# A gated linear-attention kernel with a squareplus MLP: one Softplus for the first gates, fp32 products for three cumulative sums, identity products, output column halves, and a new order table

## The chip, the cores and the metric

The kernel runs on one core of one Trainium2 chip. The metric is device time in microseconds (us) of one execution, lower is better; the time given for a kernel is the median of its runs. Engines in this text: PE is TensorE (PEld its weight loads), DVE is VectorE, ACT is ScalarE, POOL is GpSimd, SP is SyncE.

## The reference

Inputs are q, k, v and f_logit of shape (4, 8, 768, 48) in fp32, and two weight matrices, (384, 2048) and (2048, 384). The first stage is a recurrence per batch and head, the second a two-layer MLP over the 3072 tokens:

```python
f = 1.0 / (1.0 + np.exp(-f_logit))
for t in range(S):
    state = f[:, :, t, :, None] * state + einsum('bhd,bhe->bhde', k[:, :, t], v[:, :, t])
    y[:, :, t] = einsum('bhd,bhde->bhe', q[:, :, t], state)
x = y.transpose(0, 2, 1, 3).reshape(B * S, H * D)
h = x @ w_in
g = 0.5 * (h + np.sqrt(h * h + 4.0))
out = g @ w_out
```

## The kernel before

The 3072 tokens are cut into 12 *pairs* of 256 tokens, numbered 0 to 11, three to a batch. Pair 0 is handled in two *parts* of four heads each (`FINE = [0]`), all others in one part. The work on a pair is a fixed list of *pieces*, each a few instructions, made in `describe` and named by kind, pair and part: `tp2.0` is the transpose piece of pair 2. The names that matter below:

- `lf`, `lq`, `lk`, `lv` load a pair's inputs (384 KB each, SP's queue). `wi0` to `wi3` load a quarter of w_in each, `wo0` to `wo7` an eighth of w_out each, both from POOL's queue with a cast to fp16.
- `ex` and `ln` (L180, L188, ACT): the log of the gate, as ln(1 + exp(-f)), in two passes. `ad` (L194) adds the two tokens that share a partition; `hi` (L198, the helper's cast at L135 or L137) and `lo` (L203) split the sum into two fp16 halves in the tile `hl`; `cu` (L211, L217, PE) forms cumulative sums from the two halves: two products of 384 columns with a triangular matrix, and eight narrow ones of 3 columns that give block sums.
- `c1` (L225, DVE), then `ep` and `ea` (L236, ACT): exponentials of the sums. `ge` (L259, ACT) and `gs` (L264, helper L140): the decay of a whole block, 12 numbers a partition, then a multiplication that zeroes it in the other half of the partitions. `gb` (L271): the decay across two pairs.
- `qm`, `km` (helper L140): q and k scaled by these. `vc`: v in fp16. `tp` (L295, PE) and `te` (L135 or L137): transposes of q and k and their copies out of PSUM, for pairs 0 to 3; later pairs are transposed by DMA (`tx`, L278).
- `sc` (L319), `pm` (L327, DVE): scores and their masking. `kv` (L338), `ia` (L348), `sa`, `sb`: the state. `yt` (L388), `yn` (L397): the output of the recurrence; `yc`, `xp` (L421), `xe`: its cast and transposition into the tile xT.
- `m1` (L436, PE): x times w_in, eight pieces of six products to a pair. `sq` (L445) and `rt` (L450), ACT: square and square root. `gt` (L460, DVE). `m2` (L472, PE): times w_out, eight pieces of four products of 384 columns. `ev` (helper L135 or L137): out of PSUM; `st` (L493): the store.

There is no scheduler at run time. A table, `ORDER`, lists all pieces in one row of words such as `qm2.00:P` or `cu3.0:T@3`: piece, engine (S, A, D, P, T for SP, ACT, DVE, POOL, PE) and for PE the PSUM bank. Every engine runs its pieces in the order of the table, and waits at each for what it reads and for the buffer that it writes. `TABLE:e` and `TABLE:s` load ACT's function table, for exp and ln or for sqrt. The words of a piece tell its engine, so a piece can move from one engine to another through the table alone.

## Time and profile before

| | us |
|---|---|
| median of 3 runs | 189.88 (189.34 to 190.11) |
| profiled execution, whole | 188.35 |
| its span, first to last instruction | 186.6 |
| PE, ACT, DVE, POOL busy | 167.3, 161.1, 145.1, 90.2 |

The profiled execution is 1.53 us shorter than the median. 1.75 us of it lie outside of the span. Busy time counts what an engine was occupied with; a product of PE is pipelined, so its mean duration is longer than the distance from one to the next.

### The profile page before, as it was taken

What the parts mean: (1) busy time and instruction counts of PE and PEld (TensorE: products, weight loads), DVE (VectorE), ACT (ScalarE), POOL (GpSimd) and SP (SyncE); (2) the same over time, 40 slices, a digit from 0 to 9 for tenths busy, and PEclk for the clock granted to TensorE, in tenths of its full rate; (3) what the DMA queues carried; (4) which work ended last, traced back from release to release, by engine and by line L of the source; (5) the groups of instructions that cost most, each with busy time, mean ns of one, the idle gap of its engine ahead of it and who ended that gap; (6) DMA issues with size and microseconds to landing.
All of it is one profiled execution on the core that took longest, in us unless ns stands there. A gap on an engine that the chain in (4) does not pass through costs nothing.

```text
span 186.6 us, 5571 instructions
## 1 busy us (share of the span) xinstructions
PE 167.3 (90%) x2279; PEld 123.0 (66%) x2279; DVE 145.1 (78%) x277; ACT 161.1 (86%) x268; POOL 90.2 (48%) x126
## 2 busy tenths in 40 slices
...
GB/s 132 271 261 246 226 246 247 215 218 211 264 263 208 157 98 286 128 262 175 263 168 215 293 144 97 219 164 128 197 198 132 111 86 0 18 156 169 5 77 92
DMA packets 80506, 32.88 MB, mean 176 GB/s; under 512 B 73888, under 2 KB 80448, under 8 KB 80480
## 3 DMA queue, kind: packets, MB, share of 16 engines
...
q14 instruction: 8, 0.07, 0.1%
HBM read 25.17 MB, written 4.72 MB: 160 GB/s over the span
## 4 chain that ended last, share of the span: by engine, by line
PE 48%; issue 22%; DMA 15%; POOL 6%; SPq 5%; ACT 1%; POOLq 0%
PE ps L436 20%; PE ps L472 18%; DMA q<-in_q_dram 7%; POOL qk L140 4%; DMA qkT<-qk 3%; DMA f<-in_f_logit_dram 3%; SPq L173 3%; DMA k<-in_k_dram 3%; SPq L278 2%; PE ps L319 2%; PE ps L388 2%; PE ps L338 2%; PE ps L211 1%; PE ps L397 1%; PE ps L295 1%
## 5 line engine op out<-in xcount | busy, mean ns | idle before, releaser
L460 DVE SCALAR_TENSOR_TENSOR g<-ps,r 128x512 f16<-128x512 f32 x96 | 62.1, 684 | 17.4 <-ACT r L450 17.2
L436 PE MATMUL ps<-xT,win 128*128 128x256 f16 x576 | 71.2, 273 | 2.7 <-DMA win<-in_moe_w_in_dram 1.8
L472 PE MATMUL ps<-wout,g 128*128 128x384 f16 x384 | 70.8, 326 | 0.0
L436 PEld LDWEIGHTS <-win 128*128 128x128 f16 x576 | 55.0, 98 | 13.3 <-DMA win<-in_moe_w_in_dram 2.0
L445 ACT ACTIVATE hsq<-ps 128x512 f16<-128x512 f32 x96 | 53.6, 603 | 6.5 <-PE ps L436 6.2
L450 ACT ACTIVATE r<-hsq 128x1024 f16<-128x1024 f16 x48 | 50.4, 1063 | 0.8
L472 PEld LDWEIGHTS <-g 128*128 128x128 f16 x384 | 36.0, 98 | 19.7
L327 DVE TENSOR_TENSOR pm<-ps,mask 128x512 f16<-128x512 f32 x48 | 30.3, 683 | 3.2 <-PE ps L319 3.0
L140 POOL TENSOR_TENSOR qk<-k,ep 128x384 f16<-128x384 f32 (+1 forms) x19 | 19.3, 1019 | 18.7 <-PE ps L388 10.5
L140 POOL TENSOR_TENSOR qk<-q,ea 128x384 f16<-128x384 f32 (+1 forms) x19 | 18.7, 990 | 4.0 <-ACT ea L236 2.2
L493 POOL DMA_DIRECT2D out_dram<-os x2 | 1.1, 575 | 39.0 <-ACT os L135 38.4
L211 PE MATMUL ps<-hl,tri 128*128 128x384 f16 (+1 forms) x26 | 7.4, 351 | 8.9 <-DVE hl L137 6.2
L137 POOL CAST v<-v 128x768 f16<-128x768 f32 x9 | 7.8, 862 | 14.2 <-DMA v<-in_v_dram 8.8
L194 POOL TENSOR_TENSOR ss<-s 128x384 f32<-128x384 f32 (+1 forms) x10 | 9.9, 991 | 6.0 <-ACT s L188 5.9
L180 ACT ACTIVATE f<-f 128x768 f32<-128x768 f32 (+1 forms) x13 | 10.3, 802 | 2.8 <-DMA f<-in_f_logit_dram 2.8
L137 DVE COPY os<-ps 128x384 f32<-128x384 f32 (+1 forms) x17 | 8.5, 513 | 2.9 <-PE ps L472 2.9
L203 POOL TENSOR_TENSOR hl<-ss,hl 128x384 f16<-128x384 f32 (+1 forms) x11 | 9.7, 881 | 2.0 <-DVE hl L137 1.8
L188 ACT ACTIVATE s<-f 128x768 f32<-128x768 f32 (+1 forms) x13 | 10.2, 810 | 0.3
L319 PE MATMUL ps<-qkT 48*64 48x128 f16 x384 | 8.8, 227 | 1.6 <-ACT qkT L135 0.7
L137 DVE CAST y<-ps 128x384 f16<-128x384 f32 x15 | 8.1, 551 | 2.2 <-PE ps L397 2.0
L319 PEld LDWEIGHTS <-qkT 48*64 48x64 f16 x384 | 6.4, 111 | 4.9 <-issue 1.9
L135 ACT CAST y<-ps 128x384 f16<-128x384 f32 x9 | 4.2, 475 | 5.2 <-PE ps L397 3.8
...
## 6 DMA issues: line engine op xcount, KB each, us to landing
f<-in_f_logit_dram SPq DMA_DIRECT2D x11, 384.0 KB, 5.5
k<-in_k_dram SPq DMA_DIRECT2D x11, 384.0 KB, 5.0
q<-in_q_dram SPq DMA_DIRECT2D x11, 384.0 KB, 5.5
v<-in_v_dram SPq DMA_DIRECT2D x11, 384.0 KB, 6.4
...
win<-in_moe_w_in_dram POOLq DMA_DIRECT2D x4, 384.0 KB, 7.6
...
```

What stands on the lines that cost most here:

```text
L137: eng(e).tensor_copy(out=o, in_=i)
L140: eng(e).tensor_tensor(out=o, in0=a, in1=b, op=ALU.mult)
L180: nc.scalar.activation(out=t, in_=t, func=AF.Exp, scale=-1.0)
L188: nc.scalar.activation(out=T["s", p][:, :, hs], in_=T["f", p][:, hs].rearrange("p h i d -> p i h d"), func=AF.Ln, bias=1.0)
L194: eng(e).tensor_tensor(out=T["ss", p][:, hs], in0=T["s", p][:, 0, hs], in1=T["s", p][:, 1, hs], op=ALU.add)
L319: nc.tensor.matmul(out=T["sc", p, i, h][64 * cc:64 * cc + 64, j, :], lhsT=t[r, 1, j, i, :], rhs=t[r, 0, j], start=True, stop=True)
L327: eng(e).tensor_tensor(out=T["pm", p, i, h], in0=T["sc", p, i, h], in1=K["mask"][:, i].unsqueeze(1).broadcast_to([128, 4, 128]), op=ALU.mult)
L436: nc.tensor.matmul(out=T["h", p, m][:, a], lhsT=K["win"][m // 2][:, j, m % 2 * 256 + a * 128:m % 2 * 256 + a * 128 + 128], rhs=T["xT", p][ ...
L445: nc.scalar.activation(out=T["hsq", p, r][:, a], in_=T["h", p, m].rearrange("p a c t -> p (a c t)"), func=AF.Square, scale=1.0)
L450: nc.scalar.activation(out=T["r16", p, r], in_=T["hsq", p, r], func=AF.Sqrt, scale=0.25, bias=1.0)
L460: nc.vector.scalar_tensor_tensor(out=T["g", p][:, 2 * m:2 * m + 2, :].rearrange("p a t -> p (a t)"), in0=T["h", p, m].rearrange("p a c t - ...
L472: nc.tensor.matmul(out=T["o", p, cc], lhsT=T["g", p][:, jn, cc * 128:(cc + 1) * 128], rhs=K["wout"][jn // 2][:, jn % 2, :], start=(jn == 0 ...
```

## The change

Seven things, of which the last goes through the whole table:

1. Pairs 0 and 1 (`SOFT`) get the log of the gate by one ACT pass with the function Softplus in place of `ex` and `ln`. This function has a table of its own: the program begins with `TABLE:p`, and loads `TABLE:e` after the passes of these two pairs.
2. Pairs 1, 2 and 3 (`DIRECT`) have no `hi` and `lo`. `ad` writes its fp32 sum into a padded tile s32, and `cu` multiplies that in fp32: one product of 384 columns and four of 3 columns, with fp32 copies of the two constant matrices.
3. `ge` and `gs` become one piece `gs` on ACT with two passes over the same 12 numbers; a bias of 0 or -10000 makes the zeros. `gb` is laid out accordingly.
4. 40 pieces `pw` of four products of the identity with itself (128 columns, fp16) are spread over PE's order, up to the second pair. Nothing reads them.
5. The second 128 tokens of pair 11 are multiplied by w_out in two column halves of 192, each with its own bank, `ev` and two stores; the first 128 have one `ev` and two stores. Stores of pair 11 may go out from ACT's queue as well.
6. An option to mask scores on POOL (`PMACT`) is there, with an empty list.
7. `ORDER` is new throughout, with other engines for some pieces.

```diff
+DIRECT = [1,2,3]
+SOFT = [0,1]
+NS32 = 2
+PMACT = []
+WARM = 40
...
-TABLE:e lf0.1:S lf0.0:S lf1.0:S lq0.0:S lk0.0:S lq0.1:S ex0.1:A lf2.0:S ln0.1:A ex0.0:A ad0.1:P ln0.0:A lk0.1:S ad0.0:D
+TABLE:p lf0.1:S lf0.0:S lf1.0:S lq0.0:S lq0.1:S lk0.0:S pw2:T@0 pw26:T@1 lf2.0:S pw8:T@2 ln0.0:A pw30:T@3 ln0.1:A pw36:T@4
...
+                if p in SOFT:
+                    nc.scalar.activation(out=o, in_=t, func=AF.Softplus, scale=-1.0)
+                else:
+                    nc.scalar.activation(out=o, in_=t, func=AF.Ln, bias=1.0)
...
+                if direct:
+                    o = K["s32"][p % NS32][:, hs, 0:D]
...
+                if direct:
+                    tri, ind, terms = K["tri32"], K["ind32"], [K["s32"][p % NS32]]
+                else:
+                    hl = K["hl"][p % NHL]
+                    tri, ind, terms = K["tri"], K["ind"], [hl[:, 0], hl[:, 1]]
+                z = len(terms) - 1
+                for r, t in enumerate(terms):
+                    nc.tensor.matmul(out=T["cum", p][:, h0 * D:h1 * D], lhsT=tri, rhs=t[:, hs, 0:D], start=(r == 0), stop=(r == z), skip_group_check=True)
...
-            T["gs", p] = sb("gs", p, [128, 3, 4, 2], FP32)
-            mul(e, T["gs", p], T["ge", p].rearrange("p j n -> p n j").unsqueeze(3).broadcast_to([128, 3, 4, 2]),
+            T["gs", p] = sb("gs", p, [128, 2, 4, 3], FP32)
+            for h in range(2):
+                nc.scalar.activation(out=T["gs", p][:, h].rearrange("p j n -> p (j n)"), in_=T["cum", p][:, 384:396], func=AF.Exp, scale=-1.0, bias=K["half"][:, h:h + 1])
...
+        outs = [(0, 0, DM), (1, 0, DM // 2), (1, DM // 2, DM)] if p in SPLIT_OUT else [(0, 0, DM), (1, 0, DM)]
...
+    for i in range(WARM):
+        def pw(e, bk, i=i):
+            t = ps(bk[0], [128, 128], FP32)
+            for n in range(4):
+                nc.tensor.matmul(out=t, lhsT=K["ident"], rhs=K["ident"], start=True, stop=True)
```

Three places of the order. The first is the start of ACT's row, up to the exponentials of pair 0; before (L180 is `ex`, L188 `ln`, L236 `ep` and `ea`, L259 `ge`):

```order
L569 ACT_TABLE_LOAD
L180 ACTIVATE f<-f 128x384
L188 ACTIVATE s<-f 128x2x192
L180 ACTIVATE f<-f 128x384
L188 ACTIVATE s<-f 128x2x192
L180 ACTIVATE f<-f 128x768
L188 ACTIVATE s<-f 128x768
L236 ACTIVATE ep<-ps_152 128x192
```

and after (L192 is Softplus, L142 the cast `hi0.0`, L260 `ep` and `ea`):

```order
L614 ACT_TABLE_LOAD
L192 ACTIVATE s<-f 128x2x192 x2
L142 CAST hl_91<-ss 128x4x48
L192 ACTIVATE s<-f 128x768
L612 ACT_TABLE_LOAD
L260 ACTIVATE ep<-ps_197 128x192 x2
L260 ACTIVATE ea<-cm 128x192
L260 ACTIVATE ep<-cm 128x192
```

Three passes are gone there, a cast and a table load have come in, and the table load stands between the pass over pair 1 and the first exponential of pair 0.

The second is POOL's row from the third load of w_in to `qm2`, where L140 with k or q is `km` and `qm`, L194 `ad3` and `ad4`, L137 and L203 `hi3` and `lo3`; before:

```order
L146 DMA win_110<-in_moe_w_in_dram 128x3x512
L140 TENSOR_TENSOR qk_96<-k,ep 128x4x2x48
L140 TENSOR_TENSOR gb<-gs,ge 128x8
L194 TENSOR_TENSOR ss<-s 128x384 x2
L137 CAST hl_92<-ss 128x8x48
L203 TENSOR_TENSOR hl_92<-ss,hl_92 128x8x48
L146 DMA win_112<-in_moe_w_in_dram 128x3x512
L140 TENSOR_TENSOR qk_97<-k,ep 128x4x2x48
L140 TENSOR_TENSOR gs<-ge,half 128x24 x2
L137 CAST v_602<-v 128x768
L140 TENSOR_TENSOR qk_97<-k,ep 128x4x2x48
L140 TENSOR_TENSOR qk_97<-q,ea 128x4x2x48 x2
```

and after (L147 is the same helper, L153 the load of w_in, L213 `ad4` and then `ad3`, L144 `vc1`):

```order
L147 TENSOR_TENSOR qk_96<-k,ep 128x4x2x48
L153 DMA win_119<-in_moe_w_in_dram 128x3x512
L147 TENSOR_TENSOR qk_96<-q,ea 128x4x2x48
L147 TENSOR_TENSOR qk_96<-k,ep 128x4x2x48
L153 DMA win_118<-in_moe_w_in_dram 128x3x512
L213 TENSOR_TENSOR ss<-s 128x384
L213 TENSOR_TENSOR s_1_106<-s 128x8x48
L147 TENSOR_TENSOR gb<-gs 128x8
L153 DMA win_120<-in_moe_w_in_dram 128x3x512
L147 TENSOR_TENSOR qk_97<-k,ep 128x4x2x48
L144 CAST v_753<-v 128x768
L147 TENSOR_TENSOR qk_97<-k,ep 128x4x2x48
```

`hi3`, `lo3` and two `gs` are gone from between `ad3` and `qm2`, three pieces of pair 1's q and k stand between the loads of w_in, and `ad4` stands ahead of `ad3`.

The third is PE's row around the cumulative sum of pair 1; before:

```order
L211 MATMUL ps_152<-hl_91,tri 128x192
L211 LDWEIGHTS tri
L211 MATMUL ps_193<-hl_92,tri 128x384
L211 LDWEIGHTS tri
L211 MATMUL ps_193<-hl_92,tri 128x384
L217 LDWEIGHTS hl_92
L217 MATMUL ps_193<-ind,hl_92 128x3
```

and after, where L529 is `pw`, and the fp32 products have no weight load of their own in the row:

```order
L529 LDWEIGHTS ident
L529 MATMUL ps_222<-ident 128x128
L236 MATMUL ps_229<-s_1_106,tri_109 128x384
L241 MATMUL ps_229<-ind_111,s_1_106 128x3 x4
L529 LDWEIGHTS ident
L529 MATMUL ps_247<-ident 128x128
```

One wide and four narrow fp32 products stand where two wide and eight narrow ones stood, with identity products on either side.

## Rows read from the trace of the kernel before

**Rows 1.** Busy time by stretch: length; PE, PEld, DVE, ACT, POOL us (instructions); clock, DMA share, GB/s.

```profile
21.00:32.00 11.00, 8.67 (x177) 6.55 (x171) 9.34 (x17) 10.51 (x15) 8.63 (x13) 1.00 1.17 239
32.00:66.00 34.00, 34.00 (x467) 24.73 (x460) 30.31 (x58) 33.85 (x59) 25.83 (x35) 1.00 1.09 217
66.00:72.00 6.00, 5.43 (x123) 3.93 (x124) 5.11 (x10) 5.98 (x11) 2.71 (x4) 1.00 1.16 159
72.00:130.00 58.00, 57.93 (x781) 44.34 (x772) 50.68 (x88) 56.75 (x93) 32.69 (x41) 1.00 0.97 194
130.00:160.00 30.00, 29.04 (x417) 21.02 (x415) 23.28 (x40) 21.26 (x34) 5.62 (x7) 1.00 0.55 115
```

**Rows 2.** The chain that ended last, 16 to 34 us: start, us, what.

```profile
16.80 12.77 DMA q<-in_q_dram
...
29.63 1.96 POOL qk L140 x2
```

**Rows 3.** PE's timeline from 20 us: start, us, instructions, [idle before <-releaser].

```profile
21.07 1.49 PE L436 MATMUL ps<-xT,win 128*128 128x256 f16 x12
...
24.21 1.48 PE L436 MATMUL ps<-xT,win 128*128 128x256 f16 x12 [1.05 <-DMA win<-in_moe_w_in_dram]
...
26.95 1.48 PE L436 MATMUL ps<-xT,win 128*128 128x256 f16 x12 [0.74 <-DMA win<-in_moe_w_in_dram]
...
32.27 1.47 PE L436 MATMUL ps<-xT,win 128*128 128x256 f16 x12
```

**Rows 4.** ACT's timeline: the first passes, and the table load at 23 us.

```profile
6.86 0.84 ACT L180 ACTIVATE f<-f 128x768 f32<-128x768 f32 x1 [1.29 <-DMA f<-in_f_logit_dram]
...
8.48 0.31 ACT L236 ACTIVATE ep<-ps 128x192 f32<-128x192 f32 x1
8.70 0.17 ACT L259 ACTIVATE ge<-ps 128x12 f32<-128x12 f32 x1
...
23.21 1.28 ACT L571 ACT_TABLE_LOAD   x1
24.50 1.06 ACT L450 ACTIVATE r<-hsq 128x1024 f16<-128x1024 f16 x1
```

**Rows 5.** All engines from 11 us, timeline: the masks of pair 0.

```profile
15.15 2.49 DVE L327 TENSOR_TENSOR pm<-ps,mask 128x512 f16<-128x512 f32 x4 [0.47 <-PE ps L319]
```

**Rows 6.** PE's products by form, 9.5 to 17 us: count, busy us, mean ns, idle before.

```profile
L211 PE MATMUL ps<-hl,tri 128*128 128x384 f16 x4 | 1.9, 485 | 2.6 <-ACT hl L135 2.0 <-POOL hl L203 0.6
L217 PE MATMUL ps<-ind,hl 128*128 128x3 f16 x16 | 0.8, 172 | 0.0
```

**Rows 7.** The same, 44 to 62 us.

```profile
L211 PE MATMUL ps<-hl,tri 128*128 128x384 f16 x6 | 1.5, 325 | 0.0
```

**Rows 8.** The chain that ended last, at 44 us: one cumulative sum on PE.

```profile
44.45 0.33 PE ps L211 x2
44.77 0.18 PE ps L217 x8
```

**Rows 9.** POOL's timeline, 12 to 32 us.

```profile
22.23 1.00 POOL L194 TENSOR_TENSOR ss<-s 128x384 f32<-128x384 f32 x1 [1.39 <-ACT s L188]
23.17 0.50 POOL L137 CAST hl<-ss 128x384 f16<-128x384 f32 x1
23.75 0.91 POOL L203 TENSOR_TENSOR hl<-ss,hl 128x384 f16<-128x384 f32 x1
24.61 0.80 POOL L146 DMA_DIRECT2D win<-in_moe_w_in_dram  x1
```

**Rows 10.** DMA issues at 24.6 us: count, KB, us from issue to landing.

```profile
win<-in_moe_w_in_dram POOLq DMA_DIRECT2D x1, 384.0 KB, 6.9
```

**Rows 11.** All engines from 180 us, timeline: the end of the program.

```profile
179.79 2.11 PE L472 MATMUL ps<-wout,g 128*128 128x384 f16 x12
...
181.95 0.62 DVE L137 COPY os<-ps 128x192 f32<-128x192 f32 x2 [0.94 <-PE ps L472]
182.87 0.54 POOL L493 DMA_DIRECT2D out_dram<-os  x1 [0.61 <-DVE os L137]
```

More of the change, by code (lines that the diff above doesn't have):

```diff
@@ L31 @@
-ad2.0:P te0.0.0:A te0.1.1:D c11.0:D wi0:P te0.0.1:A lk2.0:S te0.1.0:D ea1.01:A hi2.0:D sc0.1:T@45 ep1.00:A lo2.0:P ex3.0:A
-sc0.0:T@67 pm0.11:D lv1.0:S wi2:P ea1.00:A cu2.0:T@0 pm0.01:D vc0.0:A pm0.10:D wi1:P ep1.01:A lq2.0:S kv0:T@23 pm0.00:D
-ea2.01:A km1.00:P ln3.0:A c12.0:D yt0:T@57 sa0:D ep2.00:A qm1.01:D ge2:A yn0.1:T yc0.0:A km1.01:D ia0.1:T ge1:A yc0.1:A
-xp0.0:T@4 gb1:P qm1.00:D ep2.01:A xp0.1:T@6 lf5.0:S ad3.0:P xe0.0:D ea2.00:A tp1.0:T@25 xe0.1:D ex4.0:A m1.0.1:T@1 te1.1.0:D
-ln4.0:A m1.0.0:T@7 te1.0.0:D sq0.1:A ad4.0:P sc1.0:T@04 sq0.0:A sc1.1:T@65 pm1.01:D TABLE:s hi3.0:P m1.0.4:T@2 sb0:D lo3.0:P
@@ new lines @@
+ep1.00:A lk2.0:S sc0.1:T@47 vc0.0:P gs0:A vc0.1:A sc0.0:T@16 pm0.10:D cu2.0:T@2 pm0.00:D km1.00:P lv1.0:S pm0.01:D pw39:T@5
+ep2.01:A kv0:T@04 pm0.11:D wi2:P ep1.01:A pw33:T@1 ex3.0:A lq2.0:S c12.0:D yt0:T@56 qm1.00:P sa0:D pw1:T@1 gs2:A gs1:A
+pw9:T@7 yc0.0:D ea2.01:A ia0.1:T km1.01:P yn0.1:T ep2.00:A xp0.0:T@1 yc0.1:D ln3.0:A qm1.01:D wi1:P xp0.1:T@0 xe0.0:A
+tp1.0:T@73 xe0.1:A ea2.00:A pw13:T@2 lf5.0:S te1.0.0:D m1.0.1:T@5 ex4.0:A te1.1.0:D m1.0.0:T@6 sq0.1:A gb1:D pw3:T@1 ln4.0:A
+pw19:T@0 sc1.0:T@27 sq0.0:A sc1.1:T@31 ad4.0:P pm1.00:D pw10:T@0 TABLE:s m1.0.5:T@0 pm1.01:D ad3.0:P m1.0.4:T@2 sb0:D rt0.0:A
@@ new lines @@
+pm1.11:D pw35:T@7 gb2:P cu3.0:T@4 wi3:P lv2.0:S sq0.5:A gt0.1:D km2.01:P sq0.4:A pw15:T@7 pm1.10:D m1.0.3:T@1 rt0.2:A c13.0:D
+m1.0.2:T@5 gt0.0:D vc1.0:P lk3.0:S sq0.3:A pw23:T@7 gt0.5:D pw11:T@3 sq0.2:A pw27:T@7 km2.00:P kv1:T@63 gt0.4:D rt0.1:A
+ia1.0:T lq3.0:S yt1:T@70 qm2.01:P sa1:D TABLE:e yn1.0:T gt0.2:D pw34:T@2 ia1.1:T qm2.00:P yn1.1:T yc1.0:D pw4:T@6 pw21:T@2
+yc1.1:D ep3.00:A xp1.0:T@5 wo1:P tp2.0:T@62 sb1:D ea3.00:A xe1.0:D ep3.01:A wo3:P xp1.1:T@7 te2.1.0:D m1.0.7:T@0 ea3.01:A
+lf7.0:S gs3:A hi4.0:P te2.0.0:D ex5.0:A m1.0.6:T@3 wo0:P xe1.1:D sq0.7:A sc2.0:T@52 gt0.3:D sc2.1:T@46 wo2:P ln5.0:A lf6.0:S
@@ new lines, in describe, with ev @@
+                W.add(f"m2.{p}.{x}{n4}", "T", m2,
+                      reads=[f"g{p}.{2 * n4}", f"g{p}.{2 * n4 + 1}", f"wout{2 * n4}", f"wout{2 * n4 + 1}"] + ([f"o{p}.{x}{n4 - 1}"] if n4 else []),
+                      makes=[f"o{p}.{x}{n4}"], uses=[("g", p)] + ([("bank", f"o{x}.{p}")] if n4 else []),
+                      banks=[f"o{x}.{p}"] if n4 == 0 else [], mode="F", part=(d1 - d0) / DM)
+            def ev(e, bk, x=x, cc=cc, d0=d0, d1=d1, p=p):
+                if ("os", p) not in T:
+                    T["os", p] = sb("os", p, [128, 2, DM], FP32)
+                copy(e, T["os", p][:, cc, d0:d1], T["o", p, x])
```

284 lines of the change are left out of this document (144 added, 140 removed).

## The prediction

> **What bounds the kernel now.** I read the busy time by stretch first [rows 1]. From 32 us on PE is full: 34.00 of 34 us, then 57.93 of 58. Its idle time is 0.57 us at 66 to 72 and 0.96 us at 130 to 160. ACT is nearly as full (33.85 of 34, 56.75 of 58). So the program is three parts: a start in which PE waits, some 150 us in which PE streams at its own pace, and an end behind the last product. A change to the start is worth only what it moves the point from which PE no longer waits.
>
> That point is read from the chain [rows 2] and from PE's timeline [rows 3]. The chain runs over the load of pair 2's q (landed 16.80 + 12.77 = 29.57), two `qm2` on POOL (29.63 + 1.96 = 31.59), on which `tp2.0` on PE waits; the next `m1` at 32.27 starts the stretch without gaps. The other waits of PE are for w_in: 1.05 us ahead of 24.21 and 0.74 us ahead of 26.95. All of these hang on DMA, which moves 239 GB/s at 21 to 32 us [rows 1], and the bytes to be loaded by then are the same in both kernels. I take 32.27 as the mark, and follow each part to it.
>
> **Softplus and its table.** Removed: three `ex` passes of pairs 0 and 1. But ACT stood still for 1.29 us for pair 1's gates, which reach it at 6.86 [rows 4]; what is saved ahead of that is saved from waiting. Behind it comes one pass of 0.84 (the row of `ex` has that; Softplus has no row, taken as equal for the same shape) and then a table load of 1.28: 6.86 + 0.84 + 1.28 = 8.98, where the first exponential stood at 8.48. So pair 0 is 0.5 us later here, not earlier. The row at 23.21 shows that a load costs no more than its 1.28: the next pass starts at 24.50.
>
> The Trainium skill says otherwise (ScalarE: Activation LUTs, section What ACT_TABLE_LOAD costs): a switch costs the load and a drain of about the same length, 2.66 us together. By that the first exponential would stand 1.4 us later still; this trace does not agree, and the sum goes by the row.
>
> **Identity products and the clock.** In the clock column the start reads 1.00 like the rest, but the products say that it ran at the lower level: one of 384 columns took 485 ns at 9.5 to 17 us and 325 at 44 to 62 [rows 6, 7]. The difference, 160 ns, is what 384 columns take more at 1.2 than at 2.4 GHz. PE had done little until then. With 32 identity products ahead of the first sum, and more in the gaps, I expect the full level by about 10 us. On pair 0's path this shortens the transposes behind the last scaled q or k (16 of 64 columns, 0.43 us at 160 ns to 384 columns) and the first half of the scores (about as much). From -0.85, the 0.5 above and the last scaled half of q, now behind another piece on POOL, I keep -0.3 for the first mask, which was at 15.15 [rows 5]. The four masks (2.49) stay.
>
> **fp32 sums.** `hi` and `lo` go for pairs 1 to 3, POOL's being 0.50 + 0.91 for pair 3 [rows 9]. On PE a sum in halves takes 0.33 + 0.18 = 0.51 us [rows 8]. fp32 products have no row. From below: one product for two and four for eight at fp16's pace, 0.25 us. From above: both operands split in two, so four wide and sixteen narrow products, 4 x 0.163 = 0.65, and the narrow ones at the busy time per product that they showed early on, 0.8 / 16 = 0.05 to twice that [rows 6]: 0.65 + 0.8 to 0.65 + 1.6, at most 2.3 us. I take 1.3, near the lower of these two, since the data are twice as wide and the level is then the full one.
>
> The Trainium skill (FP8 and Floating Point Precision, section TensorE Precision Notes) has true fp32 at four passes through the array. By that the wide product alone takes 0.65 us, twice what its two halves take: it speaks against this part of the change, and makes the lower end unlikely. No row here shows it.
>
> Where this falls: pair 2's sum stands between the scores of pair 0 and `kv0`. From about 15.1 us to the end of the masks (14.85 + 2.49 = 17.35) PE has 2.2 us, of which `kv0` and two `pw` take 0.9. Up to 1.3 us it is hidden; beyond, `yt0`, pair 0's casts, and ACT's `ep2` that waits for the sum all move one for one. With 1.3, the first `m1` comes at 20.7 to 21.0 against 21.07 [rows 3].
>
> **21 to 32 us.** Eleven `pw` stand here: 44 products of 128 columns at 0.163 / 3 = 0.054 us, 2.4 us. With `cu3` 0.8 longer that is 3.2 us more work for PE, which was idle for 11.00 - 8.67 = 2.3 us [rows 1]. They lie largely in the waits: three of them (0.65) ahead of the `m1` at 24.21 with its wait of 1.05, `cu3` and two `pw` in that of 0.74 ahead of 26.95. The second does not quite fit; the third quarter of w_in landing a little earlier (less of pair 2's inputs stands ahead of it) pays for it.
>
> POOL decides then. Before, `ad4` began at 22.23, when ACT gave `ln4`, and `hi3`, `lo3` and the issue of `wi3` at 24.61 followed [rows 9]. After, `ad4` stands ahead of `ad3`, and `ln4` on ACT stands behind the first `sq`: I put it about 1 us later, 23.2. Then two sums of 1.00 and a `gb` (0.2): `wi3` at 25.4, that is 0.8 later than 24.61, though 1.4 us of work are gone. It lands 6.9 us after its issue [rows 10], at 32.3, and the `m1` that reads it stood at 32.27. `qm2` ends at 25.4 + 0.8 + five pieces of about 1 us = 31.1 against 31.6. Both sides cancel: **0.0 us at the mark**, with bounds -1.0 (`ln4` on time, `wi3` and `qm2` both 1.4 us of POOL's work earlier, as far as PE's own work lets them) and +1.4 (fp32 at 2.3 us: `cu3` delays the `m1` behind it by 1, and `m1.0.1` is late as well).
>
> **The long stretch.** PE's work from the mark is the same. `gs` on ACT adds twelve short passes of at most 0.17 us [rows 4], 2.0 us; four `yc` casts of 384 columns moved to DVE take 1.2 to 2.5 off (192 columns took 0.31 in the row of `ep`). Taken: 0. The new order can open or close waits like the 0.57 and 0.96 [rows 1]: -1.0 to +1.5.
>
> **The end.** The last piece of PE is now half as wide, with one cast behind it instead of two on DVE, one after the other, 0.62 together [rows 11]: -0.3. The last store is half as large: 0 to -0.3. Taken: -0.35. The product of the columns is split, not enlarged, and costs PE nothing.
>
> **Sum.** 188.35 (the profiled execution) + 0.0 + 0 - 0.35 = 188.0. The median lies 1.53 above that execution; carried over, 189.88 - 0.35 = **189.5 us**.
>
> **The rivals.** *Faster*: POOL's 1.4 us come through, `wi3` is not late, and the mark moves by about -1.0; with the end, and half of the later waits gone (-0.5), 188.0. For it: POOL is on the chain [rows 2], and `hi3`, `lo3` stood ahead of both of its later steps. Against: `ad4` waits for ACT, which is 10.51 of 11 us busy there [rows 1]. *Slower, by the fp32 sums*: they take over 2 us each, so the masks no longer hide pair 2's, and `cu3` holds the `m1` behind it: mark +1.4, end -0.35, 190.9; to 192 if the level of the clock is still the lower at pair 2's. The point is 1.3 us for `cu2`. *Slower, by the order*: waits of 1.5 us or more open in the long stretch, above all where transposes by DMA are waited for: 191.0. *The identity products don't raise the clock* earlier: then they take 0.43 us a piece and stand in front of pair 0's transposes, pair 0 is 0.9 late, and it ends like the second: 190.8.
>
> **How the numbers follow.** Forecast 0.37; faster 0.34; fp32 0.13; order 0.09; clock 0.07. About 0.5% (0.95 us) is what can be told from no change. The forecast's own spread reaches over it at neither end by much, so: faster 0.34, same 0.38, slower 0.28. The range takes in the faster case down to 187.6 and the slower ones to 191.6.
>
> **What would show it.** Right: first exponential at about 9.0; wide fp16 sums at 325 ns already for pair 0; first `m1` within 0.4 us of 21.07; `m1.0.6` or its neighbour at 32.3, behind `wi3`; 4.3 us from the last product to the end. Wrong: `cu2` over 1.3 us with `yt0` behind it; `qm2` ending before 30.5; PE idle by over 2.7 us after 33 us.

## The result, and the profile after

The changed kernel takes **191.84 us** (median of 4 runs, 190.26 to 193.04) against 189.83 (189.34 to 190.11) for the kernel before, run beside it: a ratio of 1.0139, 95% interval 1.0095 to 1.0183. It is slower by 2.0 us; the forecast was 189.5, and the time lies just above its range (187.6 to 191.6). Ratios here and below leave out runs over 1.5% above a kernel's fastest; for two variants (c4_pair1_dve, g1_14_pieces) that leaves out most of them, so there the median of all runs is given too.

The profiled execution took 190.26 us with a span of 188.5 (before 188.35 and 186.6). The loss is there ahead of the mark, the `m1` from which PE no longer waits: it stood at 32.27 [rows 3] and stands at 34.52, +2.25. From the mark to PE's end it was 149.64 us and is 150.00, +0.36. From there to the end of the span it was 4.67 and is 3.97, -0.70. Together +1.91. The profiled execution is the shortest of the four runs; the other three left no trace, so this is the account of the shortest.

The busy time by stretch shows what fills the start. Of before, and then of after (columns as in [rows 1]):

```profile
21.00:32.27 11.27, 8.94 (x180) 6.77 (x175) 9.61 (x17) 10.78 (x16) 8.90 (x14) 1.00 1.16 238
21.07:32.27 11.20, 8.87 (x178) 6.76 (x175) 9.61 (x17) 10.71 (x16) 8.90 (x14) 1.00 1.16 238
32.27:180.00 147.73, 146.12 (x1911) 108.45 (x1909) 120.35 (x212) 133.22 (x217) 66.59 (x84) 1.00 0.83 166
```

```profile
21.00:34.52 13.52, 12.52 (x246) 10.62 (x247) 10.28 (x20) 12.92 (x20) 10.49 (x14) 1.00 1.13 229
22.12:34.52 12.40, 11.68 (x219) 9.93 (x218) 9.77 (x19) 11.80 (x17) 9.96 (x13) 1.00 1.12 227
34.52:180.00 145.48, 144.04 (x1897) 107.31 (x1895) 119.08 (x213) 135.40 (x222) 60.50 (x71) 1.00 0.87 165
```

From 21 us to the mark PE is busy for 12.52 us instead of 8.94, 3.58 more, and idle for 1.00 instead of 2.33. But not all of the 3.58 is added work: most of pair 1's transposes lie behind 21 us now and lay ahead of it before. It is clearer to part the 2.25 at the first `m1`. 1.05 of it arises ahead of the first `m1`, which stands at 22.12 instead of 21.07. The other 1.20 arises between it and the mark, where PE is busy for 11.68 us instead of 8.87, 2.81 more, and idle for 0.72 instead of 2.33: the old waits took in 1.61. PE's timeline of the kernel after (start, us, instructions, idle before; L529 is an identity piece, L236 and L241 the fp32 sums, L314 the transposes, L462 the `m1`, L364 `kv1`):

```profile
9.97 1.72 PE L529 MATMUL ps<-ident 128*128 128x128 f16 x28
...
14.70 0.91 PE L236 MATMUL ps<-s,tri 128*128 128x384 f32 x2
15.45 0.95 PE L241 MATMUL ps<-ind,s 128*128 128x3 f32 x8
16.26 0.38 PE L529 MATMUL ps<-ident 128*128 128x128 f16 x4
...
21.29 0.52 PE L314 MATMUL ps<-ident,qk 64*128 64x64 f16 x24 [1.09 <-DVE qk L147]
21.74 0.40 PE L529 MATMUL ps<-ident 128*128 128x128 f16 x4
22.12 1.47 PE L462 MATMUL ps<-xT,win 128*128 128x256 f16 x12
23.43 0.61 PE L529 MATMUL ps<-ident 128*128 128x128 f16 x8
...
25.65 1.48 PE L462 MATMUL ps<-xT,win 128*128 128x256 f16 x12 [0.72 <-DMA win<-in_moe_w_in_dram]
...
27.20 0.86 PE L236 MATMUL ps<-s,tri 128*128 128x384 f32 x2
27.90 0.95 PE L241 MATMUL ps<-ind,s 128*128 128x3 f32 x8
28.71 0.38 PE L529 MATMUL ps<-ident 128*128 128x128 f16 x4
28.93 1.47 PE L462 MATMUL ps<-xT,win 128*128 128x256 f16 x12
30.24 0.83 PE L529 MATMUL ps<-ident 128*128 128x128 f16 x12
31.00 0.52 PE L364 MATMUL ps<-v,qk 64*128 64x96 f16 x16
...
33.77 0.64 PE L314 MATMUL ps<-ident,qk 64*128 64x64 f16 x32
34.35 0.34 PE L447 MATMUL ps<-ident,y 128*128 128x128 f16 x3
34.52 1.47 PE L462 MATMUL ps<-xT,win 128*128 128x256 f16 x12
```

The identity pieces of the stretch in one row (products by form, 22.12 to 34.52 us, kernel after; count, busy us, mean ns, idle before):

```profile
L529 PE MATMUL ps<-ident 128*128 128x128 f16 x45 | 3.8, 219 | 0.0
```

Three things are to be seen. A sum in fp32 holds PE from 14.70 to 16.26, 1.56 us, where two halves held it for 0.51 [rows 8]; pair 3's holds it from 27.20 to 28.71. Ahead of the first `m1` stands a wait of 1.09 us for pair 1's scaled q. And between the first `m1` and the mark stand identity pieces for which PE never waits; `tp2.0` at 33.77 follows PE's own work, not POOL's `qm2`, which ended at 32.01. The 3.8 us of these pieces is busy time, in which the end of one product overlaps with the start of the next: of PE's row the twelve products at 30.24 take 0.76 us, to 31.00.

How the 1.20 adds up is seen from start to start; before, `kv1` (L338) stood here:

```profile
28.54 0.52 PE L338 MATMUL ps<-v,qk 64*128 64x96 f16 x16
```

The second group of `m1` comes 3.53 us behind the first (before 3.14), since its quarter of w_in landed later. The third comes 3.28 behind the second (before 2.74), with an fp32 sum and two identity pieces in place of a wait of 0.74. `kv1` comes 2.07 behind the third (before 1.59), with the twelve identity products ahead of it and no wait to take them in. From `kv1` to the mark it is 3.52 (before 3.73): the pieces behind `kv1` delayed nothing.

The 1.05 ahead of the first `m1` has two reasons that end together. The wait of 1.09 has its own row. All engines at 19 us, timeline of after:

```profile
19.33 1.90 DVE L147 TENSOR_TENSOR qk<-q,ea 128x384 f16<-128x384 f32 x1
...
19.80 1.00 POOL L147 TENSOR_TENSOR qk<-k,ep 128x384 f16<-128x384 f32 x1
```

DVE's multiplication takes 1.90 us where the same form alone takes 0.55 (rows of e3_pair1_dve below): it ends 0.43 us after POOL's ends. The Trainium skill (GPSIMD Engine Reference, section Specifications) says that POOL's SBUF interfaces are shared with VectorE, with contention where a DVE instruction has two inputs in SBUF. The trace agrees, with 1.90 against 0.55.

The other reason is on ACT. The first `m1` also reads xT, and its copies out of PSUM (`xe`), which DVE made before, are on ACT now, behind the log pass of pair 3 (L194). Before, and then after:

```profile
19.90 0.67 DVE L137 COPY xT<-ps 128x384 f16<-128x384 f16 x2
```

```profile
20.45 0.87 ACT L194 ACTIVATE s<-f 128x768 f32<-128x768 f32 x1
21.19 0.88 ACT L142 COPY xT<-ps 128x384 f16<-128x384 f16 x2
```

They end at 22.07, so without the wait of 1.09 the first `m1` could have started 0.05 us earlier and no more. In c1_win_first and g1_14_pieces below it does wait for these copies. No run moved them back to DVE and nothing else, so what they cost by themselves is not shown.

The end, all engines from 179 us, timeline of after; it answers to [rows 11]:

```profile
183.24 0.36 DVE L144 COPY os<-ps 128x192 f32<-128x192 f32 x1 [1.89 <-PE ps L499]
...
184.56 0.32 ACT L142 COPY os<-ps 128x192 f32<-128x192 f32 x1 [1.83 <-PE ps L499]
184.90 0.50 SPq L517 DMA_DIRECT2D out_dram<-os  x1
```

One cast of 0.32 and one store are left behind the last product (before: 0.62 on DVE, then a store from POOL).

### The profile page after: what moved, and what is told of

Same layout as the page of the kernel before. It is cut to its first block, busy times and chain, and to the rows that moved or that the text cites. A ratio compares the mean times of both kernels' runs of the same rounds, so it can differ in the third digit from the quotient of the medians.

```text
span 188.5 us, 5911 instructions
## 1 busy us (share of the span) xinstructions
PE 177.2 (94%) x2455; PEld 135.0 (72%) x2455; DVE 144.6 (77%) x278; ACT 164.1 (87%) x276; POOL 86.0 (46%) x113
## 4 chain that ended last, share of the span: by engine, by line
PE 31%; ACT 25%; issue 24%; DVE 7%; DMA 6%; POOL 4%; POOLq 0%; SPq 0%; ACTq 0%; DVEq 0%
PE ps L462 11%; PE ps L499 11%; ACT hsq L471 6%; ACT r L476 5%; DMA win<-in_moe_w_in_dram 4%; DVE g L486 3%; ACT ep L260 3%; ACT ea L260 2%; ACT L616 2%; ACT L612 2%; ACT s L194 2%; PE ps L529 2%; ACT f L200 2%; PE ps L236 2%; POOL qk L147 2%
## 5 line engine op out<-in xcount | busy, mean ns | idle before, releaser
L462 PE MATMUL ps<-xT,win 128*128 128x256 f16 x576 | 70.4, 273 | 1.6 <-DMA win<-in_moe_w_in_dram 0.7
L499 PE MATMUL ps<-wout,g 128*128 128x384 f16 (+1 forms) x400 | 70.7, 320 | 0.0
L462 PEld LDWEIGHTS <-win 128*128 128x128 f16 x576 | 55.3, 98 | 11.2 <-issue 1.1
L147 POOL TENSOR_TENSOR qk<-k,ep 128x384 f16<-128x384 f32 (+1 forms) x20 | 19.9, 1001 | 7.5 <-DMA k<-in_k_dram 5.1
L147 POOL TENSOR_TENSOR qk<-q,ea 128x384 f16<-128x384 f32 (+1 forms) x18 | 17.2, 962 | 3.0 <-ACT ea L260 1.8
L529 PE MATMUL ps<-ident 128*128 128x128 f16 x160 | 13.2, 238 | 2.3 <-POOL ident masks.py:199 2.3
L529 PEld LDWEIGHTS <-ident 128*128 128x128 f16 x160 | 11.1, 109 | 2.8 <-POOL ident masks.py:199 2.3
L144 DVE CAST y<-ps 128x384 f16<-128x384 f32 x19 | 10.2, 551 | 2.0 <-PE ps L423 2.0
L147 POOL TENSOR_TENSOR sn<-st,gb 128x384 f16<-128x384 f32 x6 | 5.2, 868 | 14.3 <-DVE st L390 12.8
L147 POOL TENSOR_TENSOR sn<-st,gs 128x384 f16<-128x384 f32 x5 | 4.5, 898 | 14.5 <-DVE st L390 14.5
L144 DVE COPY os<-ps 128x384 f32<-128x384 f32 (+1 forms) x16 | 8.5, 539 | 3.1 <-PE ps L499 2.3
L213 POOL TENSOR_TENSOR ss<-s 128x384 f32<-128x384 f32 (+1 forms) x8 | 7.2, 901 | 6.8 <-ACT s L194 5.1
L142 ACT COPY os<-ps 128x384 f32<-128x384 f32 (+1 forms) x9 | 4.2, 462 | 6.2 <-PE ps L499 6.2
L200 ACT ACTIVATE f<-f 128x768 f32<-128x768 f32 x10 | 8.4, 854 | 1.0 <-DMA f<-in_f_logit_dram 1.0
L338 PE MATMUL ps<-qkT 48*64 48x128 f16 x384 | 8.4, 220 | 0.4 <-DVE g L486 0.4
```

What stands on the lines that cost most here:

```text
L144: eng(e).tensor_copy(out=o, in_=i)
L147: eng(e).tensor_tensor(out=o, in0=a, in1=b, op=ALU.mult)
L200: nc.scalar.activation(out=t, in_=t, func=AF.Exp, scale=-1.0)
L462: nc.tensor.matmul(out=T["h", p, m][:, a], lhsT=K["win"][m // 2][:, j, m % 2 * 256 + a * 128:m % 2 * 256 + a * 128 + 128], rhs=T["xT", p][ ...
L499: nc.tensor.matmul(out=T["o", p, x], lhsT=T["g", p][:, jn, cc * 128:(cc + 1) * 128], rhs=K["wout"][jn // 2][:, jn % 2, d0:d1], start=(jn = ...
L529: nc.tensor.matmul(out=t, lhsT=K["ident"], rhs=K["ident"], start=True, stop=True)
```

## The experiments

Four theories were to be told apart: the *fp32 sums* (1.5 us or more each on PE), the *clock* (whether the identity products raise it, and what they cost where they don't), *Softplus* and its table, and the *order* (handovers, loads, POOL beside DVE). Variants whose names begin with b and f stand on the order of before, the others on the new one.

### Single suspects undone in the kernel after

Loads of w_in, the third and second quarter right behind the first in POOL's order:

```diff
-POOL: wi0 vc0.0 km1.00 wi2 qm1.00 km1.01 wi1
+POOL: wi0 wi2 wi1 vc0.0 km1.00 qm1.00 km1.01
```

> The changed kernel with one change of order: POOL issues wi2 and wi1, the second and third load of w_in, right behind wi0 instead of behind the scalings of pair 1. In the changed kernel they go out at 18.02 and 20.74 us, land at 25.61 and 28.42, and m1.0.5 and m1.0.3 start at 25.65 and 28.93; the mark (first m1 behind tp2.0) is 34.52. Theory LOADS (late issue of w_in sets the mark): they land near 24.2 and 26.9 as before the change, m1.0.5 starts at 24.2, the mark comes to 33.1 and the time falls by about 1.4 us. Theory PE WORK (fp32 sums and identity products fill PE until the mark): m1.0.5 starts earlier, but the mark moves by under 0.5 us, and so does the time.

Measured: 191.59 us, ratio 1.013 (1.007 to 1.0191). The loads were asked for at 14.93 and 15.71 us and nothing was gained: their issue is not the loss. Theory PE WORK is nearer in the time, but the profile doesn't test it, as it differs from the one above in another way. PE's timeline of c1_win_first:

```profile
9.18 1.65 PE L236 MATMUL ps<-s,tri 128*128 128x384 f32 x2 [0.35 <-POOL s L213]
10.62 1.70 PE L241 MATMUL ps<-ind,s 128*128 128x3 f32 x8
12.19 3.15 PE L529 MATMUL ps<-ident 128*128 128x128 f16 x28
...
18.62 0.64 PE L338 MATMUL ps<-qkT 48*64 48x128 f16 x32
```

Here the products show the lower level up to about 17.5 us, although the same 160 identity products run. (The clock column reads 1.00 there, as it does at the start of the kernel before.) The fp32 sum holds PE for 3.01 us (9.18 to 12.19) and the 28 products behind it take 3.15 instead of 1.72; the scores of pair 0 start at 18.62 instead of 14.13, the first `m1` at 25.55, the mark is at 37.33.

The same with two multiplications of pair 1 moved to DVE as well:

```diff
-qm1.00:P km1.01:P
+qm1.00:D km1.01:D
```

> As c1_win_first, and qm1.00 and km1.01 stand on DVE behind qm1.01, as before the change; only km1.00 stays on POOL. In the changed kernel DVE's qm1.01 took 1.90 us (19.33 to 21.23) while POOL worked on km1.01. Theory COLLISION (DVE's scaling waits for POOL's): each of the three takes about 0.55 us, tp1.0 ends by 21.2 instead of 21.8, and m1.0.1 is then set by ACT's xe0.1 alone (22.07); below c1_win_first by 0 to 0.3 us. Theory LOADS: as c1_win_first. If m1.0.1 still starts at 22.1, pair 0's path over ACT is what makes it late.

Measured: 3 of 10 runs at 189.01 to 190.54 (ratio 1.0022, 0.996 to 1.0084), the others at 192.46 to 195.05; the median of all ten is 192.76. This told nothing on the collision, so it was done again without the moved loads (e3, below).

The last 12 identity pieces away:

```diff
-pw13 ... pw21 (12 pieces behind the first transposes of pair 1)
```

> The changed kernel without its last 12 identity pieces (from the transposes of pair 1 on); the 28 ahead of them stay, so the clock rises as early. They take about 0.22 us each on PE, 2.6 us together. Theory PE WORK: the 8 of them between the first m1 and tp2.0 that stand where PE does not wait are gained, the mark falls from 34.52 to about 33.0 and the time by 1.5 us. Theory LOADS: they lie in waits that return; mark and time move by under 0.5 us.

Measured: 191.73 us, 1.0134 (1.0075 to 1.0192), no gain. From the first `m1` to the mark its profile has 11.57 us (24.94 to 36.51) against 12.40 in the kernel after, so without these pieces this stretch is 0.83 us shorter in the profile. That is less than they take of PE's row: waits came back instead, 0.94 us for POOL's `ad3` and 0.78 for DVE's `yc1`, and from `kv1` to the mark it is 3.95 us. But in this execution the level fell back to the lower one from 9.5 to 16.4 us, and the first `m1` came 2.8 us later.

Sums split into fp16 halves again:

```diff
-DIRECT = [1,2,3]
+DIRECT = []
+ad1.0 hi1.0:D lo1.0:P ... ad2.0 hi2.0:D lo2.0:P ... ad3.0 hi3.0:P lo3.0:P
```

> The changed kernel with the sums of pairs 1 to 3 in two fp16 halves again: hi1, hi2 on DVE, lo1, lo2, hi3, lo3 on POOL, each right behind its ad; all else as changed. Theory PE WORK: a sum takes 0.5 us on PE instead of 1.5, so yt0, ep2 and c13 come about 1 us earlier; mark and time fall by 1.0 us or more. Theory LOADS: POOL has 3.7 us more work ahead of wi2, wi1 and wi3, these land later, and the time rises by 1 us or more.

Measured: 191.38 us, 1.0114 (1.0051 to 1.0177). The added `hi1.0` stood ahead of `c10.0` on DVE and held the first exponential to 10.14 us, so this run doesn't price the sums. With `hi1.0` behind `c10.0`, and pair 3's sum ahead of pair 4's:

```diff
-c10.0:D ... te0.0.0:D ... ad4.0:P ad3.0:P
+c10.0:D hi1.0:D lo1.0:P ... te0.0.0:D hi2.0:D ... ad3.0:P hi3.0:P lo3.0:P ad4.0:P
```

> The kernel after with the sums of pairs 1 to 3 split into fp16 halves again, the two steps of pair 1 placed behind the first half of pair 0's prefix copy on VectorE (the earlier variant with split sums had put one ahead of it, which held the first exponential back by about 1.5 us), and the sum of pair 3 prepared ahead of pair 4's. Theory FP32: three sums shorter by 0.9 us each at the full level, of which those of pairs 2 and 3 lie on the path: 190.0 us, ratio 1.003. Theory ORDER: 191.4 us or more, ratio 1.010 or more.

Measured: 191.02 us, 1.0101 (1.007 to 1.0132). By the ratio that is theory ORDER: the fp32 sums are some 0.4 points of the 1.4, but the two intervals overlap.

No identity products at all:

```diff
-pw0 ... pw39
```

> The changed kernel without any identity piece. Theory CLOCK (in the traces so far the full level comes at 5.7 us and stays, or falls again at 9.0 to 9.5, or comes only at 17.5; while it is low, the 28 identity products ahead of pair 0's transposes take 3.15 us instead of 1.72 and pair 0 is up to 4 us late): without them pair 0 runs at the lower level throughout, but nothing stands ahead of it; the first m1 starts at 22 to 23, the runs lie closer together than 190.3 to 193.0, and the median falls by 0.5 to 1.5 us. Theory PE WORK: 2.6 us of late pieces go besides, the time falls by 1.5 us or more. If the identity products were worth their place, the time rises.

Measured: 191.6 us, 1.0095 (1.0061 to 1.013). About 0.4 points better than the kernel after, with intervals that overlap too. Without them the level is the lower one up to 26.4 us and two fp32 sums lie in that time; with them it is raised early in some executions and the pieces are in the way in others.

Pair 1's multiplications on DVE, with the loads as they were:

```diff
-wi2 qm1.00:P km1.01:P wi1
+wi2 wi1
+qm1.01:D km1.01:D qm1.00:D
```

> The kernel after with the last two multiplications of q and k of pair 1 moved from GpSimd to VectorE, right behind the one that already stands there; the loads of w_in 2 and 1 on GpSimd's queue thereby come about 1 us forward. Theory COLLISION (the 1.90 us of VectorE's multiplication beside GpSimd's, and the 1.09 us that TensorE waits for it, are the loss in the order): first product of w_in 0.8 to 1.1 us earlier than in a run of the kernel after with the same clock, 190.8 us. Theory NOT THERE (something else is late next, such as w_in's landing or the first exponential of pair 3): 191.5 to 192.0 us.

Measured: 193.2 us, 1.0184 (1.0117 to 1.025): worse, if anything. DVE and PE, timelines of e3_pair1_dve:

```profile
23.25 0.55 DVE L147 TENSOR_TENSOR qk<-q,ea 128x384 f16<-128x384 f32 x1
23.71 0.55 DVE L147 TENSOR_TENSOR qk<-k,ep 128x384 f16<-128x384 f32 x1
24.18 0.55 DVE L147 TENSOR_TENSOR qk<-q,ea 128x384 f16<-128x384 f32 x1
```

```profile
24.79 0.64 PE L314 MATMUL ps<-ident,qk 64*128 64x64 f16 x32 [1.06 <-DVE qk L147]
25.36 0.40 PE L529 MATMUL ps<-ident 128*128 128x128 f16 x4
25.59 1.47 PE L462 MATMUL ps<-xT,win 128*128 128x256 f16 x12
```

The collision is gone (0.55 three times), and PE waits 1.06 us all the same, now for three multiplications in a row behind pair 0's casts. The collision is a fact of one row and not what decides.

### Single parts on the order of before

```diff
+SOFT = [0, 1]
-TABLE:e ... ex0.1:A ... ln0.1:A ex0.0:A ... ex1.0:A ... ln1.0:A
+TABLE:p ... ln0.1:A ... ln1.0:A TABLE:e
```

> The kernel before with one part of the change: Softplus for pairs 0 and 1, its table first and the exponentials' table behind pair 1's pass. The first exponential comes about 0.1 to 0.5 us later (8.59 in the changed kernel, 8.48 before) with ACT otherwise 1.9 us lighter: the time moves by -0.3 to +0.5 us in every theory; if by more, this part has a share that no theory has.

Measured: 190.7 us, 1.0097 (1.0046 to 1.0149), more than any theory had. The first exponential stood at 9.12. PE's timeline of b2_soft:

```profile
15.89 1.01 PE L217 MATMUL ps<-hl,tri 128*128 128x384 f16 x2
16.70 0.40 PE L223 MATMUL ps<-ind,hl 128*128 128x3 f16 x8
17.05 0.82 PE L344 MATMUL ps<-v,qk 64*128 64x96 f16 x16
...
21.79 2.74 PE L442 MATMUL ps<-xT,win 128*128 128x256 f16 x12 [0.23 <-DMA win<-in_moe_w_in_dram]
```

Pair 0 is 0.4 us late throughout; the larger part is the first group of `m1`, 2.74 us at the lower level where it took 1.49 in the profile of before [rows 3]. In the lower level a sum in halves takes 1.16 us (15.89 to 17.05).

```diff
+DIRECT = [1, 2, 3]
-hi1.0 lo1.0 hi2.0 lo2.0 hi3.0 lo3.0
```

> The kernel before with one part of the change: the sums of pairs 1 to 3 by fp32 products, without hi and lo; order otherwise as before, no identity products. The changed kernel's trace has 1.5 us for such a sum at the full level and 3.0 at the lower one, against 0.5 and 0.9 in halves. Theory PE WORK: pairs 1 and 2 fall in the time at the lower level, so cu1 ends 1 us and yt0 starts 1.5 us later, and the time rises by 0.8 to 1.5 us. Theory LOADS: POOL has 3.2 us less to do ahead of the loads of w_in, these go out earlier, and the time falls by up to 1 us.

Measured: 190.67 us, 1.005 (1.0015 to 1.0085), as theory PE WORK had it. PE's timeline of b3_fp32:

```profile
15.97 1.65 PE L224 MATMUL ps<-s,tri 128*128 128x384 f32 x2
17.41 1.71 PE L229 MATMUL ps<-ind,s 128*128 128x3 f32 x8
19.05 0.82 PE L350 MATMUL ps<-v,qk 64*128 64x96 f16 x16
```

The sum of pair 2 holds PE for 3.08 us, 1.9 more than the halves in b2_soft at the same level, and `kv0` starts behind it without a wait: nothing hides it.

```diff
-        for cc in range(2):
+        outs = [(0, 0, DM), (1, 0, DM // 2), (1, DM // 2, DM)] if p in SPLIT_OUT else [(0, 0, DM), (1, 0, DM)]
```

> The kernel before with one part of the change: the second 128 tokens of pair 11 in two column halves, with the stores' engines of the change. In the traces the span ends 4.67 us behind PE's last product before, and 3.97 after. All theories: the end is worth 0.5 to 0.7 us, the time falls by that.

Measured: 189.28 us, 0.9984 (0.9947 to 1.0022). From PE's end to the end of the span its profile has 3.98 us, as in the kernel after, against 4.67: the 0.7 us are there in the profile. In the time it is 0.3 us, which the interval doesn't tell from none.

```diff
+pw0 ... pw7 cu0.1 ... cu0.0 pw8 ... pw11 ... cu1.0 pw12 ... pw15
```

> The kernel before with 16 pieces of four identity products and nothing else: eight ahead of the first sum of pair 0, four behind its second sum, four behind the sum of pair 1. Theory CLOCK (identity products raise the clock early, and the transposes and scores of pair 0 at the full level bring the first product of w_in 0.5 to 1 us forward): 188.6 to 189.2 us, full level in the records before 12 us. Theory WORK (where the clock has not risen, a piece takes 0.43 us of TensorE's queue ahead of the transposes, and the products are in the way): 190.0 to 191.0 us, first product of w_in later than 21.07 us. If they only fill waits: 189.6 us.

Measured: 188.89 us, 0.9952 (0.9907 to 0.9997), below before, on the edge of the interval. The time is that of theory CLOCK; the profile is not: its clock column is at 0.50 from 9.5 to 23.1 us, and the first `m1` is at 22.31, which theory WORK had. With the halves too:

```diff
+pw0 ... pw15
+        outs = [(0, 0, DM), (1, 0, DM // 2), (1, DM // 2, DM)] if p in SPLIT_OUT else [(0, 0, DM), (1, 0, DM)]
```

> The kernel before with the 16 early pieces of identity products and the column halves at the end, no Softplus, no fp32 sums, the old order. Theory CLOCK: 0.3 us under the kernel before with identity products alone, 188.3 to 188.9 us. Theory WORK: 189.7 us or more. The halves alone gave 0.998 of the time before.

Measured: 188.41 us, 0.9931 (0.9894 to 0.9969), **faster than both kernels**. Theory CLOCK in the time; yet its profile has the full level only from 14.0 to 17.5 and from 24.3 us, so that the profile does not show how those 1.2 us come about.

### Parts together, and the order alone

The arithmetic of before in the new order:

```diff
-SOFT = [0,1]
+SOFT = []
-DIRECT = [1,2,3]
+DIRECT = []
-pw0 ... pw39
+ad1.0 hi1.0:D lo1.0:P ... ad2.0 hi2.0:D lo2.0:P ... ad3.0 hi3.0:P lo3.0:P
```

> The kernel after with the arithmetic of before: exponential and logarithm for pairs 0 and 1, sums split into two fp16 halves, no identity products. Left of the change are the new order, the scale by one activation per half, and the column halves at the end. Theory PARTS (the time went into Softplus, alone +1.0 %, and the fp32 sums, alone +0.5 %; order and identity products together are worth nothing): 189.3 us, 188.7 to 189.9, the third group of products behind w_in 3 by about 32.3 us of the profile. Theory ORDER (the new order itself loses: VectorE waits beside GpSimd for the scaled k of pair 1, and w_in 1 and 2 are asked for 2 to 4 us later): 190.4 us or more, the first product of w_in not before 21.8 us.

Measured: 193.18 us, 1.0201 (1.0133 to 1.0268). This looks like ORDER, but as in c3 the added `hi1.0` on DVE held `c10.0` to 10.32 and the first exponential to 11.44, 3 us later than before. It is no clean test of the order. The other way round is: the parts added to the old order, on top of b5_pw_halves.

```diff
+SOFT = [0, 1]
```

> The old order with 16 early identity pieces and the column halves (0.993 of the time before, 188.4 us), and Softplus for pairs 0 and 1 added. Theory PARTS (each part costs what it cost alone on the old order; Softplus alone +1.0 %): 1.003 of the time before, 190.2 us. Theory TABLE ONLY (what Softplus costs is the 0.4 to 0.65 us by which the first exponential of the kernel comes later, the rest of its +1.0 % was a first group of products at the lower clock): 0.996, 188.9 us.

```diff
+DIRECT = [1, 2, 3]
```

> The old order with 16 early identity pieces and the column halves, and the sums of pairs 1 to 3 by fp32 matmuls added, the six steps of the split gone. Theory PARTS (+0.5 % as alone): 0.998, 189.3 us. Theory FP32 ON THE PATH (a sum takes 1.5 us of TensorE at the full level and 3.1 us at the lower one, against 0.6 and 1.2 for the halves, with nothing to cover the sum of pair 2, which stands between the scores and the products of pair 0): 1.001 to 1.006, 189.8 to 190.8 us, where the records show the lower level at the sums of pairs 1 and 2.

```diff
+SOFT = [0, 1]
+DIRECT = [1, 2, 3]
```

> The old order with 16 early identity pieces, the column halves, Softplus and the fp32 sums: all parts of the change but the new order, the scale by activations and 24 of the identity pieces. Theory PARTS (0.993 + 1.0 % + 0.5 %): 1.008, 191.1 us, and the new order would then be worth +0.4 % of the 1.2 to 1.4 % by which the kernel after is slower. Theory ORDER (the new order is what loses, the parts together cost little once the clock is raised early): 1.000 or less, 189.6 us or less.

| on the order of before | median us | ratio to before (95%) |
|---|---|---|
| 16 pieces, halves (b5) | 188.41 | 0.9931 (0.9894 to 0.9969) |
| and Softplus (f1) | 188.32 | 0.9938 (0.9893 to 0.9983) |
| and fp32 sums (f2) | 190.16 | 1.0033 (0.9995 to 1.007) |
| and both (f3) | 188.78 | 0.9981 (0.9947 to 1.0015) |
| the kernel after | 191.84 | 1.0139 (1.0095 to 1.0183) |

Softplus costs nothing here (f1 beside b5), so the 1.0% that it cost alone is not its price beside the identity pieces; why is not shown. The fp32 sums cost 0.4 points (f3 beside f1, whose intervals overlap) to 1.0 (f2 beside b5, as theory FP32 ON THE PATH had it). And all parts together are no slower than the kernel before; the theory PARTS (1.008) fell, and theory ORDER held, with its condition that the clock is raised early. What lies between 0.998 and 1.014 is the new table, with 24 more identity pieces and the scale by activations: **1.6 points, 3 us**.

This comparison has identity pieces on both sides. Without any, the new table is at 1.0095 (d1), and Softplus, the fp32 sums and the halves, each alone on the order of before, multiply to 1.0131 (1.0097 x 1.005 x 0.9984). So without pieces the record shows no loss by the order. The order of before with these three parts and no pieces was not run. It may be that the old table gains by its 16 pieces what the new one doesn't gain by its 40.

What in the table? The 26 later of its 40 identity pieces away:

```diff
-pw31 pw25 pw20 ... (all behind pw5, the fourth piece behind pair 1's sum)
```

> The kernel after with only its first 14 identity pieces of 40 (eight ahead of pair 0's sums, two behind them, four behind pair 1's sum); the 26 behind them, which stand between the sums, transposes, scores and products up to 33 us, are gone. Theory PIECES (these 26 are the loss of the new order: they are queued ahead of work whose operands are there, 0.43 us each at the lower level and 0.2 at the full one): as all parts on the old order, 1.004 of the time before or less, 190.2 us or less, and the mark at most 33.5 us. Theory HANDOVERS (the steps that changed engines and places are the loss): 1.010 or more, 191.2 us or more.

Measured: 4 of 12 runs at 188.61 to 190.29 (ratio 1.0025, 0.9988 to 1.0062), eight at 191.68 to 193.68; the median of all is 191.72. PE's timeline of g1_14_pieces, an execution of 188.61 us:

```profile
14.93 0.91 PE L234 MATMUL ps<-s,tri 128*128 128x384 f32 x2
15.68 0.95 PE L239 MATMUL ps<-ind,s 128*128 128x3 f32 x8
16.56 0.77 PE L362 MATMUL ps<-v,qk 64*128 64x96 f16 x16
...
20.20 1.03 PE L312 MATMUL ps<-ident,qk 64*128 64x64 f16 x32
21.39 2.48 PE L460 MATMUL ps<-xT,win 128*128 128x256 f16 x12 [0.15 <-ACT xT L140]
...
33.43 1.47 PE L460 MATMUL ps<-xT,win 128*128 128x256 f16 x12
```

The wait of 1.09 ahead of the transposes of pair 1 is not there, the first `m1` is at 21.39, and the mark at 33.43, 1.1 us ahead of the kernel after, although the level was the lower one from 16.7 to 23.5 us. So the new table can run as fast as the old one without those pieces. It mostly did not: theory PIECES fits a third of the runs, theory HANDOVERS the rest. Each run's mean granted clock is on record beside its time: 0.962 to 1.000 in the four shorter runs, 0.954 or 0.955 in six of the eight longer ones, 0.995 and 1.000 in the other two. A run of 0.954 is profiled below (g2_14_swap); its clock column shows 0.50 for 17.1 us in all, against 6.8 here. So the long runs go mostly with long falls of the clock; that the falls make them long is not shown, and in b5_pw_halves means of 0.959 to 0.989 went with 187.18 to 189.10 us.

And with the handovers of pair 0 as before:

```diff
-yc0.0:D yc0.1:D xe0.0:A xe0.1:A ... yc0.1:D qm1.01:D
+yc0.0:A yc0.1:A xe0.0:D xe0.1:D ... sa0:D qm1.01:D ... wi0:P wi2:P wi1:P
```

> As the kernel with 14 pieces, and the old handovers between 17 and 22 us: pair 0's copies of y on ScalarE and of x transposed on VectorE as before, the multiplication of q of pair 1 on VectorE ahead of them, and the loads of w_in 2 and 1 right behind w_in 0 on GpSimd. Theory HANDOVERS: 0.8 to 1.2 us less than with 14 pieces alone. Theory PIECES: within 0.4 us of it.

Measured: 192.56 us, 1.0186 (1.0134 to 1.0237), worse. HANDOVERS fell, at least in this form, as far as one can tell beside the clock: PE waited 0.72 us ahead of pair 1's transposes, for ACT's decay passes, and this execution had the lower level at 8.8 to 15.6 and 19.0 to 29.3 us.

**What stays open.** With identity pieces in the program, the same arithmetic costs nothing in the old table and 1.4 points in the new one: that much is shown. Whether the order by itself loses or only its identity pieces and what the clock makes of them is not shown, nor which of its moves it is: the loads, the collision, the handovers and the last 12 pieces were undone one at a time and none gave it back; the 26 pieces gave it back in 4 runs of 12. What the traces show beside it is that the level of the clock at 9 to 25 us differs from run to run of one kernel, and that a table with more of PE's work in that time has more to lose by it: from the start of pair 1's fp32 sum to the end of the 28 products behind it PE takes 3.2 us in the kernel after (8.41 to 11.62) and 6.1 in c1_win_first (9.18 to 15.27). That this alone makes the 1.6 points is argued, not shown.

## Why the prediction was wrong, step by step

- **The first `m1`** was forecast at 20.7 to 21.0 and stood at 22.12: the first of two steps that failed, 1.05 of the 2.25 us. Up to pair 0's first mask the forecast was right (14.85; it was at 14.59). Behind the masks the sum took over the path of the kernel before and had no term for the pieces that changed engines and places there: ACT's copies of x, which end at 22.07, and pair 1's last multiplication on DVE, which ends at 21.23.
- **21 to 32 us** is the other, 1.20 of the 2.25 us. The prediction counted 3.2 us more work for PE against 2.3 us of idle time, said itself that this doesn't quite fit, and took 0.0 at the mark, since w_in would land earlier and POOL decided. Measured from the first `m1` to the mark: PE busy for 2.81 us more, 1.61 of idle time taken in. The size of the identity pieces was about right (twelve products in 0.76 us, 0.063 each, forecast 0.054); where their time would go was not. The third quarter of w_in landed at 28.42, 1.5 us later, not earlier. POOL was later too (the issue of `wi3` at 26.59, forecast 25.4; `qm2` done at 32.01, forecast 31.1), and yet didn't decide, as `tp2.0` stood in PE's own queue until 33.77. A wait that was idle before covers added work only where the work stands right ahead of it: ahead of `kv1` there were twelve identity products and no wait.
- **The fp32 sum** was put at 1.3 us, hidden up to 1.3. It holds PE for 1.56 us at the full level, inside of the bounds of 0.25 to 2.3, and for 3.0 to 3.1 at the lower one, outside. The wide product alone went from 14.70 to 15.45, 0.75 us, against 0.163 for one of its two halves. The Trainium skill (FP8 and Floating Point Precision, section TensorE Precision Notes) has four passes for fp32, which makes 0.65 us for the wide product (an estimate, 4 x 0.163); the trace agrees as to its size. The prediction, which named it, took too low a value for the whole. At the lower level nothing hid the sum of pair 2 (b3_fp32); in the profiled execution `yt0` behind it came at 17.35, earlier than before (17.70).
- **The clock** rose early in the profiled execution (full level from 5.7 us), as forecast. But of 14 profiled kernels with identity products the level stayed up in two only, the kernel after and f2; in the others it came late or fell back within 3 to 11 us. "Full level by about 10 us" was taken as a fact of the kernel, and it is one of the run. The rival that named this (190.8) was given 0.07.
- **Softplus**: first exponential forecast at 8.98; it stood at 8.59 in the kernel after, 9.12 in b2_soft and 8.99 in f1_b5_soft. The term was right on the order of before; in the kernel after, pair 1's pass began at 6.44 and not at 6.86. What it is worth in the time is about 0.1 us (f1 beside b5). The load took 1.28 us again, and the next pass began right behind it (7.30 + 1.28 = 8.58, then 8.59).
- **The long stretch** was put at 0 and gave +0.36. **The end** was put at -0.35 and gave -0.70.
- **The rivals**: slower came, and by none of them as written. The fp32 sums have some 0.4 points, as far as intervals that overlap can tell. The table has the rest, but its loss arose ahead of the mark, not in the long stretch where the rival by the order had put it. The rival of the clock had its level right in most profiles, its cost not shown. That the mark sets the end one for one holds only to about 1 us: f2_b5_fp32 had its mark at 33.99, 1.72 later than before, and a span of 186.5, as PE was idle for 0.50 us behind the mark and not 1.61, and the end was 0.7 shorter.
